# Sliding-window score products over 96 and 100 rows in place of 128 zero-padded rows

## The chip, the cores and the metric

The kernel runs on one core of one Trainium2 chip. A core has five engines with their own instruction streams: TensorE (PE in the profile: matmuls, with its weight loads listed apart as PEld), VectorE (DVE), ScalarE (ACT), GpSimd (POOL), and SyncE (SP), which here issues most DMA transfers. The metric is the device time of one execution in microseconds.

## The reference: what is computed

The input x has 2048 positions of 512 features. Two branches are computed from it and mixed by a gate.

```
a = real(DFT_seq(DFT_hidden(x)))                 # two dense matrix products, real part
q, k, v = x @ wqkv                               # 32 heads of 16
scores = q k^T / 4, masked to 0 <= query - key < 256
b = softmax(scores) @ v, heads joined, @ wo
g = sigmoid(sum(x * gate_w))
out = g * a + (1 - g) * b
```

All numbers are float32.

## The kernel before, in words

A float32 operand x is split into hi, its rounding to the matmul's own format (fp32r), and lo = x - hi; a product is then the sum of hi·hi, hi·lo and lo·hi. The dense products (projections of q, k and v in lines 259 to 313, the hidden DFT in line 320, the sequence DFT in line 520, and the output product in line 785) run these three terms as three matmuls of 128x128 weights against 512 columns.

The attention does the three terms in one matmul, by stacking them along the contracted rows. The 32 heads are worked in four groups, each with four pairs of heads. For a pair there are 32 features (two heads of 16). Two large tiles, called rings, hold 2048 positions for the four pairs: ring 0 holds queries, scaled and with the sign turned, with rows 0 to 31 hi, 32 to 63 lo and 64 to 95 hi again; ring 1 holds keys with rows 0 to 31 hi, 32 to 63 hi and 64 to 95 lo. The 96 rows thus give hi·hi + lo·hi + hi·lo. `ring_load` (line 286) fills 512 positions of both rings with four DMA transfers from a scratch in DRAM.

For a block n of 64 positions, `make_pad` (line 334) builds the stationary operand from a ring: a pad holds the 64 positions twice, once with the rows of one head of the pair and zeros in those of the other, and once the other way round, so that its 128 columns are two heads times 64 positions. `s_pair` (line 353) multiplies a pad of queries with a window of ring 1, at most 320 keys; DVE adds the mask and takes the row extreme (line 365), ACT takes the exponential and its sum (line 368). These give each query's extreme and sum. `t_pair` (line 432) later multiplies a pad of keys with a window of ring 0, at most 320 queries, which gives the scores transposed; the extremes of the two heads are brought back by DMA into rows 96 to 99 of ring 0 (`m_ring`, line 401, hi and lo for two heads), and rows 96 to 99 of the key pads hold ones for the head that a column belongs to, so that the matmul itself takes the extreme into the score. ACT takes the exponential (line 446), POOL clears what lies outside the window (lines 450 and 454), and `pv` (line 457) multiplies with the values in plain float32, in four column strips of the array (128x32 each).

In the kernel before, both score products read all 128 rows of pad and ring. Rows that hold nothing must then be zero. There are two pads of queries, two of keys, and the two rings:

- The query pads' rows 96 to 127 are cleared once by POOL (`affine_select` in line 203). It reads a split tile of x only to have something to read; the result is zero throughout.
- The rings' rows 96 to 127 are cleared by POOL in eight pieces of 512 positions (`clear_rows`, line 197, called ahead of the loop and at n = 1, 3 and 5).
- The key pads' rows 96 to 127 are set to one by POOL and multiplied on DVE by the columns of `mrow` (`clear_pads`, line 209, called at n = 7). `mrow` is one in rows 96 and 97 for one head, 98 and 99 for the other, and zero elsewhere, so rows 100 to 127 become zero.

The order of PE's work is written out in the program: the loop over n (line 844) issues `s_pair` of block n for the four pairs, `t_pair` of block n - 19, and between them `fill` takes pieces of the stream of dense work (`dense`, line 586), so that one score product stands between every two or three dense matmuls. After the loop the rest of the dense work follows, then the output product. The order of POOL and of most of DVE and ACT is set by a scheduler from the program's dependencies, within the bounds of `behind` (a given instruction stays after another). The first loads and splits of the program (from line 144) are in a written order on DVE, ACT and SP.

Of the kernel before, what the change touches and what calls it, by code (L numbers as in the profile page):

```python
# [10 lines left out]
OP = mybir.AluOpType  # L11
# [3 lines left out]
P = 128  # L15
# [4 lines left out]
NP = 4  # L20
# [12 lines left out]
def fnet_window_mix(ctx: ExitStack, tc: tile.TileContext, xT, x, wqk, wv, wr, wi, cr, ci, wo, gw, out):  # L33
    nc = tc.nc
# [23 lines left out]
    def f(ap):  # L58
        return ap.bitcast(F32)
# [4 lines left out]
    def mark(e, ins):  # L64
        last[e] = ins.ins

    @contextmanager
    def behind(*engines):
        with ExitStack() as es:
            for e in engines:  # L70
                if e in last:
                    es.enter_context(tc.issue_after(last[e]))
            yield
# [50 lines left out]
    XT = {}  # L124
# [17 lines left out]
    with tc.manual_schedule(engines={mybir.EngineType.Activation, mybir.EngineType.DVE, mybir.EngineType.SP}):  # L142
# [12 lines left out]
        for dk in range(DK):  # L155
            c = slice(dk * 256, dk * 256 + 256)
# [6 lines left out]
    pads = [[const.tile([P, NP, P], F32R, name=f"pad{i}_{b}") for b in range(NPAD)] for i in range(2)]  # L163
    ring = [const.tile([P, NP, S], F32R, name=f"ring{i}") for i in range(2)]
# [3 lines left out]
    for h in (0, 64):  # L168
        m = mask[h:h + 64, :]
        nc.gpsimd.affine_select(m, m, pattern=[[1, WIN]], compare_op=OP.is_gt, fill=BIG,  # L170
                                base=0, channel_multiplier=-1)
        nc.gpsimd.affine_select(m, m, pattern=[[-1, WIN]], compare_op=OP.is_ge, fill=BIG,
                                base=256, channel_multiplier=1)
# [3 lines left out]
                            base=0, channel_multiplier=-1)  # L177
# [3 lines left out]
    mrow = const.tile([P, 2], F32, name="mrow")  # L181
    for t, edges in ((half, ((0, 16, 32, 48, 64, 80), (16, 32, 48, 64, 80, 96))), (mrow, ((96, 98), (98, 100)))):
        nc.gpsimd.memset(t, 0.0)
        for h in range(2):
            for i, e in enumerate(edges[h]):
                a = t[:, h:h + 1]
                nc.gpsimd.affine_select(a, a, pattern=[[0, 1]], compare_op=OP.is_ge, fill=1.0 - i % 2,
                                        base=e - 1, channel_multiplier=-1)
# [5 lines left out]
    def turned(t):  # L194
        return t[:].rearrange("x p (r h) -> x p r h", h=2)

    def clear_rows(i, ss):
        with behind("pool"):
            nc.gpsimd.memset(f(ring[i][96:128, :, ss * 512:(ss + 1) * 512]), 0.0)

    first_lo = f(XT[0, 0][96:128, 1]).rearrange("r (p c) -> r p c", p=NP)
    for t in pads[0]:
        mark("pool", nc.gpsimd.affine_select(t[96:128], first_lo, pattern=[[0, NP], [0, P]], compare_op=OP.is_gt,
                                             fill=0.0, base=0, channel_multiplier=0))
    clear_rows(1, 0)
    clear_rows(0, 0)
    vpad = [const.tile([P, 4, NP, 32], F32, name=f"vpad{b}") for b in range(2)]

    def clear_pads():
        for t in pads[1]:  # L210
            nc.gpsimd.memset(f(t[96:128]), 1.0)
            for h in range(2):
                a = turned(t)[96:128, :, :, h]
                nc.vector.tensor_scalar(a, f(a), mrow[96:128, h:h + 1], None, op0=OP.mult)


    gl = const.tile([P, 16], F32, name="gl")
# [114 lines left out]
    PAD = {}  # L332

    def make_pad(i, n):
        if not 0 <= n < NG * NB:
            return
        t = pads[i][n % NPAD]
        b = n % NB
        with behind(*(("act", "dve") if n < NPAD else ())):
            for h in range(2):  # L340
                src = f(ring[i][:96, :, b * BQ:(b + 1) * BQ])
                dst = turned(t)[:96, :, :, h] if i else t[:96, :, 64 * h:64 * h + 64]
                if i and h:
                    nc.scalar.activation(dst, src, AF.Copy, scale=half[:96, h:h + 1])  # L344
                else:
                    nc.vector.tensor_scalar(dst, src, half[:96, h:h + 1], None, op0=OP.mult)  # L346
        PAD[i, n] = t
# [5 lines left out]
    def s_pair(n, p):  # L353
        j = n % NB
        u, jj = divmod(n, 8)
        if jj == 0 and p == 0:
            ML[u] = at.tile([P, 2, NP * 8], F32, name="ml")
        nm, l = ML[u][:, 0], ML[u][:, 1]
        k0 = max(0, (j - 4) * BQ)
        w = (j + 1) * BQ - k0  # L360
        c = slice(p * 8 + jj, p * 8 + jj + 1)
        ps = ps_a.tile([P, 512], F32, name="s", tag="st")
        nc.tensor.matmul(ps[:, :w], PAD[0, n][:, p], ring[1][:, p, k0:k0 + w], start=True, stop=True)  # L363
        sm = at.tile([P, WIN], F32, name="sm", bufs=3)
        mark("dve", nc.vector.tensor_tensor_reduce(out=sm[:, :w], in0=ps[:, :w], in1=mask[:, WIN - w:],  # L365
                                                   scale=1.0, scalar=3e38, op0=OP.add, op1=OP.min,
                                                   accum_out=nm[:, c]))
        mark("act", nc.scalar.activation(sm[:, :w], sm[:, :w], AF.Exp, bias=nm[:, c], scale=-1.0,  # L368
                                         accum_out=l[:, c]))
# [52 lines left out]
    def v_spread(n):  # L422
        if n >= NG * NB:
            return
        raw = VR.pop(n)
        v2 = vpad[n // 4 % 2]
        for h in range(2):
            nc.gpsimd.tensor_scalar(v2[:, :, :, 16 * h:16 * h + 16], raw.rearrange("r j (p d) -> r j p d", d=16),  # L428
                                    side[:, h:h + 1], None, op0=OP.mult)
        V2[n // 4] = v2  # L430

    def t_pair(n, p):
        q0 = n % NB * BQ
        w = min(WIN, S - q0)
        if p == 0:
            if "proj" in have:
                more.append(n)
            c = (n - more[0]) % 6 * NP * WIN if more else 3072
            if c + NP * WIN <= 3072:
                PT[n] = f(home[:, c:c + NP * WIN].rearrange("p (a b) -> p a b", a=NP))  # L440
            else:
                PT[n] = at.tile([P, NP, WIN], F32, name="pt", bufs=4)
        pt = PT[n]
        ps = ps_a.tile([P, 512], F32, name="t", tag="st")
        nc.tensor.matmul(ps[:, :w], PAD[1, n][:, p], ring[0][:, p, q0:q0 + w], start=True, stop=True)  # L445
        nc.scalar.activation(pt[:, p, :w], ps[:, :w], AF.Exp, scale=-1.0)  # L446
        if p % 2:
            ph = slice(p - 1, p + 1)
            a = pt[:, ph, 0:64]
            nc.gpsimd.affine_select(a, a, pattern=[[0, 2], [2, 64]], compare_op=OP.is_ge, fill=0.0,  # L450
                                    base=1, channel_multiplier=-1)
            if w == WIN:
                a = pt[:, ph, 256:320]
                nc.gpsimd.affine_select(a, a, pattern=[[0, 2], [-2, 64]], compare_op=OP.is_gt, fill=0.0,  # L454
                                        base=-1, channel_multiplier=1)
# [352 lines left out]
    def ring_ahead(n):  # L808
        nonlocal loaded
        while loaded < 16:  # L810
            g, ss = divmod(loaded, 4)
            if n >= 32 * g + 8 * ss:
                need(("qk", g, ss))
            if ("qk", g, ss) not in have or n - LAG < 32 * (g - 1) + 8 * ss + 9:
                break
            with behind(*(("sp",) if g == 0 else ())):
                ring_load(g, ss)
            loaded += 1
# [18 lines left out]
    def v_next(n):  # L837
        if n < N:
            for c in range(2):
                need(("v", n % NB // 2 + c))  # L840
            with behind(*(("sp",) if n < 8 else ())):
                v_load(n)

    for n in range(N + LAG + 1):
        if n in (1, 3, 5):
            for i in range(2):
                clear_rows(1 - i, (n + 1) // 2)
        if n == 7:
            clear_pads()
        k = n - LAG  # L850
        ring_ahead(n + 1)
        if k in (-1, 4):
            v_spread(0 if k < 0 else 4)
        if k in (-4, -1, 4):
            v_next({-4: 0, -1: 4, 4: 8}[k])
        if n == 0:
            make_pad(0, 0)
        for p in range(NP):
            if n < N:
                s_pair(n, p)  # L860
            fill(n)
            if 0 <= k < N:
                t_pair(k, p)
            if p == 0:
                make_pad(0, n + 1)
                if k >= -1:
                    make_pad(1, k + 1)
            fill(n)
            for at_n, at_p, do in TURN:
                u, j = divmod(n - at_n, 8)  # L870
                if p == at_p and j == 0 and 0 <= u < 16:
                    do(u)
            if p == 3 and k % 8 == 6 and 0 <= k < N:
                l_load(k // 8)
            if p == 0 and full:
                o_out()
            if p == 2 and (k - summed >= (5 if more else 3) or k == N):
                for j in range(summed, k):
                    pv(j)
                summed = k  # L880
            if p == 3 and 4 * spread - 5 < summed and 4 * spread < N and n >= fresh:
                v_spread(4 * spread)
                spread += 1
                v_next(4 * spread)
                fresh = n + 2
# [49 lines left out]
```

## Time and profile before

| what | value |
|---|---|
| three runs | 858.51, 852.27 and 853.18 us, median 853.18 |
| the profiled execution | 854.57 us, with a span of 852.9 us from first to last instruction |
| PE busy | 844.8 us (99% of the span), 5166 matmuls |
| PEld busy | 691.3 us (81%) |
| DVE, ACT, POOL busy | 615.8, 593.7 and 251.9 us |
| score products, lines 363 and 445 | 512 each, mean 308 and 301 ns |
| mean granted clock of TensorE | 1.00 |

The profile is of one execution. A row of a group has the line of the program, engine, operation, what it writes and reads, the shape and the count; then busy time and mean duration, then the idle time just ahead of it on its engine. In PE's rows "128*128" is active rows times active columns of the array. Matmuls overlap in the array: one starts while the one before it still drains, so the time that a matmul takes from PE is read from its start to the next one's start, and not from its duration. In a timeline, rows of a kind that follow on each other are merged into one with a count, and idle time is in brackets with what ended it.

### The profile page before, as it was taken

The page shows a single profiled execution, that of the slowest core. Times are in us where ns is not written, and L with a number is a line of the kernel's source. Part 1 is how long each engine was busy: PE and PEld are TensorE (multiplying, and loading weights), DVE is VectorE, ACT ScalarE, POOL GpSimd, SP SyncE. Part 2 cuts the span into 40 slices and gives each one's busy share as a digit, 9 for nine tenths or more (in the row PEclk, how much of TensorE's full clock was granted, in tenths as well). Part 3 has the DMA queues.
Part 4 walks back from the last instruction along what each step waited for, and adds up shares of the span by engine and source line. Part 5 has one row for each costly group of instructions (what it writes and reads, how often), then busy time and mean ns, then how long its engine had stood idle before and what let it go on. Part 6 is the DMA issues. An engine that isn't in the chain of part 4 may idle for free.

```text
span 852.9 us, 16687 instructions
## 1 busy us (share of the span) xinstructions
PE 844.8 (99%) x5166; PEld 691.3 (81%) x5166; DVE 615.8 (72%) x2013; ACT 593.7 (70%) x1793; POOL 251.9 (30%) x585
## 2 busy tenths in 40 slices
PE   9999999999999999999999999999999999999998
PEld 7788788788788888888878887888888887877887
DVE  5588978667878787669777787788888774437531
ACT  5388798878888987779878897778777765532200
POOL 9000222333332333333423324333243354510000
PEclk9999999999999999999999999999999999999999
DMA  7876578576675275444435557989784344359542
GB/s 255 276 235 201 172 247 249 198 236 210 205 249 181 59 210 127 152 125 143 148 120 145 164 144 216 286 278 292 242 225 140 117 153 144 124 176 303 158 147 98
DMA packets 94344, 160.99 MB, mean 189 GB/s; under 512 B 26800, under 2 KB 35760, under 8 KB 94256
## 3 DMA queue, kind: packets, MB, share of 16 engines
q1 hardware_dynamic: 93824, 159.28, 59.8%
q8 instruction: 40, 0.66, 0.3%
q10 hardware_dynamic: 432, 0.66, 0.2%
q14 instruction: 48, 0.39, 0.1%
HBM read 108.27 MB, written 51.64 MB: 187 GB/s over the span
## 4 chain that ended last, share of the span: by engine, by line
PE 92%; DMA 4%; DVE 2%; ACT 1%; issue 1%; SPq 0%; DVEq 0%; ACTq 0%
PE dc L523 39%; PE dab L300 10%; PE s L363 9%; PE t L445 8%; PE o L471 8%; PE dqk L277 8%; PE t L793 5%; PE dv L300 4%; DMA raw<-xT 1%; DMA fin<-o_scr 1%; DMA o_scr<-ev 1%; DVE sm L365 1%; DMA pt<-wqk 0%; DVE big L81 0%; SPq L56 0%
## 5 line engine op out<-in xcount | busy, mean ns | idle before, releaser
L368 ACT ACTIVATE sm<-sm,ml 128x320 f32<-128x320 f32 (+4 forms) x512 | 277.9, 544 | 101.1 <-DVE ml L365 96.4
L523 PE MATMUL dc<-big,hi 128*128 128x512 f32 x1020 | 344.4, 393 | 0.0
L365 DVE CUSTOM_DVE_ANT_0 sm<-s,mask 128x320 f32<-128x320 f32 (+4 forms) x512 | 235.3, 464 | 113.2 <-PE s L363 91.5
L523 PE MATMUL dc<-big,lo 128*128 128x512 f32 x510 | 200.6, 393 | 0.0
L523 PEld LDWEIGHTS dc<-big,hi 128*128 128x128 f32 x1020 | 179.7, 188 | 21.4
L446 ACT ACTIVATE pt<-t 128x320 f32<-128x320 f32 (+4 forms) x392 | 160.3, 411 | 43.0 <-PE t L445 40.9
L450 POOL TENSOR_SCALAR_AFFINE_SELECT pt<-pt 128x128 f32<-128x128 f32 x196 | 72.2, 368 | 302.0 <-ACT pt L446 299.8
L363 PE MATMUL s<-ring,pad 128*128 128x320 f32 (+4 forms) x512 | 157.7, 308 | 0.0
L445 PE MATMUL t<-ring,pad 128*128 128x320 f32 (+4 forms) x512 | 154.1, 301 | 0.1
L346 DVE TENSOR_SCALAR pad<-ring,half 96x256 fp32r<-96x256 f32 x384 | 119.9, 358 | 13.5 <-PE t L445 13.3
L363 PEld LDWEIGHTS s<-ring,pad 128*128 128x128 f32 x512 | 96.1, 188 | 30.3 <-issue 9.0
L445 PEld LDWEIGHTS t<-ring,pad 128*128 128x128 f32 x512 | 96.1, 188 | 22.0 <-DVE ml L365 1.0
L523 PEld LDWEIGHTS dc<-big,lo 128*128 128x128 f32 x510 | 95.9, 188 | 13.8 <-issue 1.6
L368 ACT ACTIVATION_READ_ACCUMULATOR sm<-sm,ml 128x1 f32 x512 | 97.7, 191 | 0.0
L428 POOL TENSOR_SCALAR vpad<-vr,half 128x256 f32<-128x256 f32 x64 | 60.5, 958 | 124.9 <-DMA vr<-v_scr 75.7
L579 DVE TENSOR_TENSOR lo<-raw,hi 128x512 fp32r<-128x512 f32 x142 | 96.8, 691 | 0.1
L300 PE MATMUL dab<-hi,big 128*128 128x512 f32 x256 | 89.2, 394 | 0.0
L277 PE MATMUL dqk<-big,hi 128*128 128x512 f32 x240 | 85.7, 394 | 1.5 <-DVE big L81 0.9
L579 DVE CAST hi<-raw 128x512 fp32r<-128x512 f32 x142 | 60.1, 432 | 18.7 <-PE dc L523 13.0
L344 ACT ACTIVATE pad<-ring,half 96x256 fp32r<-96x256 f32 x128 | 66.6, 520 | 0.0
L454 POOL TENSOR_SCALAR_AFFINE_SELECT pt<-pt 128x128 f32<-128x128 f32 x172 | 62.0, 361 | 0.1
L446 ACT ACTIVATE home<-t 128x320 f32<-128x320 f32 (+4 forms) x120 | 49.0, 408 | 13.4 <-PE t L445 11.5
(97 smaller groups left out, 915.3 us busy)
## 6 DMA issues: line engine op xcount, KB each, us to landing
qk_scr<-home SPq DMA_DIRECT2D x32, 512.0 KB
ring<-qk_scr SPq DMA_DIRECT2D x32, 512.0 KB
raw<-cr SPq DMA_DIRECT2D x32, 512.0 KB
raw<-ci SPq DMA_DIRECT2D x32, 512.0 KB
r_scr<-ev SPq DMA_DIRECT2D x42, 256.0 KB
ev<-r_scr SPq DMA_DIRECT2D x42, 256.0 KB
ab_scr<-home SPq DMA_DIRECT2D x20, 512.0 KB
big<-ab_scr SPq DMA_DIRECT2D x20, 512.0 KB
```

Source lines behind the costliest of these rows:

```text
L277: nc.tensor.matmul(ps, w[a][:, c:c + 128], XT[dk, ss][:, b], start=n == 0, stop=n == 11)
L300: nc.tensor.matmul(ps, XT[dk, ss][:, a, c * 128:(c + 1) * 128], wh[b], start=n == 0, stop=n == 11)
L346: nc.vector.tensor_scalar(dst, src, half[:96, h:h + 1], None, op0=OP.mult)
L363: nc.tensor.matmul(ps[:, :w], PAD[0, n][:, p], ring[1][:, p, k0:k0 + w], start=True, stop=True)
L365: mark("dve", nc.vector.tensor_tensor_reduce(out=sm[:, :w], in0=ps[:, :w], in1=mask[:, WIN - w:], scale=1.0, scalar=3e38, op0=OP.add, op1= ...
L368: mark("act", nc.scalar.activation(sm[:, :w], sm[:, :w], AF.Exp, bias=nm[:, c], scale=-1.0, accum_out=l[:, c]))
L445: nc.tensor.matmul(ps[:, :w], PAD[1, n][:, p], ring[0][:, p, q0:q0 + w], start=True, stop=True)
L446: nc.scalar.activation(pt[:, p, :w], ps[:, :w], AF.Exp, scale=-1.0)
L450: nc.gpsimd.affine_select(a, a, pattern=[[0, 2], [2, 64]], compare_op=OP.is_ge, fill=0.0, base=1, channel_multiplier=-1)
L471: nc.tensor.matmul(OT[g, sb][32 * p:32 * p + 32, q - sb * 512:e - sb * 512], v2[:, p], pt[:, p, q - q0:e - q0], start=first, stop=kb == 8 ...
L523: nc.tensor.matmul(ps, w[a][:, i % 8 * 128:i % 8 * 128 + 128], ab[SC[i]][:, b], start=i == ends[0] and a + b == 0, stop=i == ends[1] and a ...
L579: return fn(*args)
```

## The change

The score products read 96 rows of query pad and ring 1 (`s_pair`), and 100 rows of key pad and ring 0 (`t_pair`). Nothing reads the other rows any more, so the clearing of the query pads and of both rings is taken out, and that of the key pads is cut to rows 96 to 99.

```diff
-    def clear_rows(i, ss):
-        with behind("pool"):
-            nc.gpsimd.memset(f(ring[i][96:128, :, ss * 512:(ss + 1) * 512]), 0.0)
-
-    first_lo = f(XT[0, 0][96:128, 1]).rearrange("r (p c) -> r p c", p=NP)
-    for t in pads[0]:
-        mark("pool", nc.gpsimd.affine_select(t[96:128], first_lo, pattern=[[0, NP], [0, P]], compare_op=OP.is_gt,
-                                             fill=0.0, base=0, channel_multiplier=0))
-    clear_rows(1, 0)
-    clear_rows(0, 0)
...
         for t in pads[1]:
-            nc.gpsimd.memset(f(t[96:128]), 1.0)
+            nc.gpsimd.memset(f(t[96:100]), 1.0)
             for h in range(2):
-                a = turned(t)[96:128, :, :, h]
-                nc.vector.tensor_scalar(a, f(a), mrow[96:128, h:h + 1], None, op0=OP.mult)
+                a = turned(t)[96:100, :, :, h]
+                nc.vector.tensor_scalar(a, f(a), mrow[96:100, h:h + 1], None, op0=OP.mult)
...
-        nc.tensor.matmul(ps[:, :w], PAD[0, n][:, p], ring[1][:, p, k0:k0 + w], start=True, stop=True)
+        nc.tensor.matmul(ps[:, :w], PAD[0, n][:96, p], ring[1][:96, p, k0:k0 + w], start=True, stop=True)
...
-        nc.tensor.matmul(ps[:, :w], PAD[1, n][:, p], ring[0][:, p, q0:q0 + w], start=True, stop=True)
+        nc.tensor.matmul(ps[:, :w], PAD[1, n][:100, p], ring[0][:100, p, q0:q0 + w], start=True, stop=True)
...
-        if n in (1, 3, 5):
-            for i in range(2):
-                clear_rows(1 - i, (n + 1) // 2)
```

In the changed program PE, ACT and SP have the same instructions in the same order, apart from the rows. The four multiplies of `clear_pads` on DVE, which the scheduler places, move from behind the splits of the second quarter of x to just behind the first split of the first weights (line 159).

## The prediction

> **What bounds the kernel now.** I read the page first (span, busy slices, chain of waits), then the busy time by stretches, then the order of instructions in time where the kinds of product meet.
>
> ```profile
> span 852.9 us, 16687 instructions
> PE   9999999999999999999999999999999999999998
> PEclk9999999999999999999999999999999999999999
> PE 92%; DMA 4%; DVE 2%; ACT 1%; issue 1%; SPq 0%; DVEq 0%; ACTq 0%
> L363 PE MATMUL s<-ring,pad 128*128 128x320 f32 (+4 forms) x512 | 157.7, 308 | 0.0
> L445 PE MATMUL t<-ring,pad 128*128 128x320 f32 (+4 forms) x512 | 154.1, 301 | 0.1
> ```
>
> ```profile
> 0.00:35.00 35.00, 32.21 (x129) 25.38 (x130) 19.35 (x38) 13.97 (x25) 21.84 (x41) 1.00 0.85 282
> 119.00:340.00 221.00, 221.00 (x1440) 180.13 (x1440) 172.91 (x599) 186.64 (x580) 70.25 (x176) 1.00 0.61 192
> 340.00:689.00 349.00, 349.00 (x2282) 287.86 (x2281) 275.38 (x958) 273.19 (x856) 116.63 (x276) 1.00 0.60 183
> ```
>
> The columns of the second view are the length of the stretch, then busy time and count of PE, PEld, DVE, ACT and POOL, the granted clock, the DMA share and GB/s. In the two long stretches that hold most of the attention PE has no idle time, at a granted clock of 1.00; DVE and ACT sit at 78% and 84% of 119 to 340 us (172.91 and 186.64 of 221). So the kernel ends when PE has got through its list, and a change counts by what it adds to or takes from PE's slots. The exception is the first 26 us, where PE waits for inputs. The 1024 score products (512 in line 363, 512 in line 445) are what the change touches on PE. Their durations overlap, so their price must be read from starts:
>
> ```profile
> 126.90 0.31 PE L363 MATMUL s<-ring,pad 128*128 128x320 f32 x1
> 127.04 0.39 PE L300 MATMUL dab<-hi,big 128*128 128x512 f32 x1
> 127.27 0.39 PE L300 MATMUL dab<-lo,big 128*128 128x512 f32 x1
> 127.50 0.31 PE L445 MATMUL t<-ring,pad 128*128 128x320 f32 x1
> 127.64 0.62 PE L300 MATMUL dab<-hi,big 128*128 128x512 f32 x2
> ```
>
> A score product of 320 columns holds PE for 0.14 us (126.90 to 127.04, and 127.50 to 127.64), a dense one of 512 for 0.23 us. That is 0.44 and 0.45 ns a column: the slot goes with the moving columns, which the change leaves alone.
>
> **The change part by part.** The changed program has the same matmuls in the same order on PE; 512 of them have 96 rows and 512 have 100 in place of 128, and all 1024 keep the 128x128 tile at position 0, with the same moving columns and the same 128 stationary columns. The issues of SP and ACT are the same and in the same order, so no transfer passes another.
>
> *(a) 1024 products of fewer rows.* The trace has no product or weight load with fewer than 128 rows, so this is the unknown price. Bound from below: if a slot went with its rows, it would fall by 0.14 x 32/128 = 0.035 us for 512 of them and by 0.14 x 28/128 = 0.031 us for the other 512, 34 us in all. Nothing excludes that; the slots above follow columns, but at one number of rows. For the bound from above there are two places where another number of active columns enters PE:
>
> ```profile
> 133.87 0.39 PE L300 MATMUL dab<-hi,big 128*128 128x512 f32 x1
> 133.88 0.36 PEld L383 LDWEIGHTS s<-ident,mlh 128*64 128x64 f32 x2
> 134.10 0.28 PE L383 MATMUL s<-ident,mlh 128*64 128x128 f32 x2
> 134.22 0.36 PE L363 MATMUL s<-ring,pad 128*128 128x320 f32 x1
> ```
>
> ```profile
> 118.42 0.67 PE L300 MATMUL dab<-hi,big 128*128 128x512 f32 x2
> 119.02 1.82 PE L471 MATMUL o<-pt,vpad 128*32 128x320 f32 x24
> 120.77 0.41 PE L363 MATMUL s<-ring,pad 128*128 128x320 f32 x1
> 121.02 0.39 PE L300 MATMUL dab<-lo,big 128*128 128x512 f32 x1
> ```
>
> In the first, from 128*128 to 128*64 and back, the weights of the small product load while the dense product streams (133.88, just after 133.87); the dense product takes its usual 0.23 us, and the two small ones of 128 columns take 0.12 us together, 0.06 each, by columns again. This border costs nothing. In the second, from 128*128 to 128*32 with plain f32 operands, two dense products take 0.60 us (118.42 to 119.02) where 0.46 is usual, 0.14 us more; on the way back the score product holds PE for 0.25 us where 0.14 is usual, 0.11 us more. There the next weights were not loaded under the product in flight. Paying 0.14 + 0.11 at both borders of each of 1024 products would be 512 us: the upper end. I take zero, by the first border: it is nearest, since it keeps the operands' type and the same place in the array, as the change does, and changes only how much of the array is active.
>
> The Trainium skill ("TensorEngine Tiling (Array Packing)", Key Properties) says that changing the tiling mode, not just the tile, drains the array. By that rule the 128*64 border ought to drain as well, and this trace shows it does not; the 128*32 border agrees. The page's modes have 128, 64 or 32 rows, so 96 and 100 rows would stay in the 128-row mode and the rule would give no change; were 96 rows a mode of their own, it would give the 512 us of the upper end. The skill also says ("TensorE: Matmul & The Clock Gate", LDWEIGHTS) that a weight load costs by columns and a 32-row load takes as long as a 128-row one; no run here shows that yet, and it would give zero too.
>
> *(b) Clearing that goes.* POOL loses the eight ring clears and the two selects that clear the first pads.
>
> ```profile
> 5.86 0.32 POOL L187 TENSOR_SCALAR_AFFINE_SELECT mrow<-mrow 128x1 f32<-128x1 f32 x2
> 6.25 1.23 POOL L203 TENSOR_SCALAR_AFFINE_SELECT pad<-big 32x512 fp32r<-32x512 f32 x2
> 7.42 14.09 POOL L199 MEMSET ring<- 32x2048 f32 x8
> 21.85 0.32 POOL L187 TENSOR_SCALAR_AFFINE_SELECT mrow<-mrow 128x1 f32<-128x1 f32 x2
> ```
>
> ```profile
> L363 PE MATMUL s<-ring,pad x512: 191/310/418, 35.0 to 688.1; 128*128 128x320 f32 x149, 128*128 128x64 f32 x6, 128*128 128x256 f32 x6, 128*128 128x128 f32 x5
> ```
>
> These 15 us end at 21.5 us; the first score product is at 35 us and waits on loads into its ring, so the clears are hidden and their going is worth zero in itself.
>
> *(c) The key pads' multiplies move on DVE.* There are still four of 256 elements a row, now on 4 rows instead of 32; I price them the same, since the elements in a row set the work. Their inputs (mrow, line 187) come earlier because POOL is free, and they move from 24.9 us to DVE's place just after its first line 159:
>
> ```profile
> 5.45 0.42 DVE L159 TENSOR_TENSOR lo<-pt,hi 128x256 fp32r<-128x256 f32 x1
> 6.94 1.07 DVE L81 TENSOR_TENSOR big<-pt,big 128x512 fp32r<-128x512 f32 x1 [1.08 <-ACT big L78]
> ...
> 8.28 0.68 DVE L81 TENSOR_TENSOR big<-pt,big 128x512 fp32r<-128x512 f32 x1
> ```
>
> ```profile
> 11.46 3.57 DMA raw<-xT
> ...
> 24.92 0.35 DVE pad L214
> ...
> 25.31 0.70 DVE big L81
> ...
> 26.05 3.47 PE dqk L277 x14
> ```
>
> In the changed order the multiplies wait for the second pair of mrow selects. These end 0.66 us after the clears (22.17 against 21.51), and now follow at once on the first pair, which ends at 6.18: about 6.8 us. Four multiplies of up to 0.35 us end at about 8.1. Queued behind them is the split of line 81 that began at 6.94, for which PE waits: 1.2 us late. It took 1.07 us beside POOL's selects against 0.68 for the next, so without them it gets 0.39 back: 0.8 us late. The splits behind it stand close, and the raw buffer that the transfer at 11.46 refills is freed by the last of them, so the delay runs along this chain (views: DVE's order in time, then the chain of waits). Further on, the 0.35 us multiply between two splits (0.39 us from its start to the next split's) has gone. Net: +0.8 - 0.4 = +0.4 us at 26.05, where PE takes over and carries it to the end. Bounds: -0.8 if all of the wait is hidden (0.39 + 0.39), +1.2 if nothing is given back.
>
> **Sum.** 0 (a) + 0 (b) + 0.4 (c): a span of 853.3 us against 852.9. The profiled execution took 854.57 us, 1.4 more than the median of the three runs, 853.18; against the median I forecast **853.6 us**.
>
> **Rivals.**
>
> *Weights not loaded ahead (slower).* If PE does not load weights for another number of rows while a product streams, the load is exposed at each entry, as at 120.77. Place: each of the 1024 products; price: 0.11 us, 113 us, 967 us. For it: that border exists. Against: 128*64 shows no such thing. It decides from 8 ns a product (8.5 us).
>
> *Drain at both borders (slower).* Entry and exit both pay, 0.11 to 0.25 us each: +225 to +512 us, 1079 to 1366 us. Same evidence, and a stronger claim.
>
> *A small fee (slower).* Something of 0.01 to 0.03 us a product, too small for the starts to show at the 128*64 border: +10 to +31 us, 864 to 885 us.
>
> *Rows count (faster).* The lower bound of (a): up to 34 us, 820 us; half of it, 837 us, if only one of weight load and stream shortens. Against it: the weight loads follow columns, and lie under the stream anyway:
>
> ```profile
> L445 PEld LDWEIGHTS t<-ring,pad 128*128 128x128 f32 x512 | 96.1, 188 | 22.0 <-DVE ml L365 1.0 <-PE s L363 0.3
> L383 PEld LDWEIGHTS s<-ident,mlh 128*64 128x64 f32 x32 | 4.3, 134 | 3.1 <-DVE mlh L377 1.0
> ```
>
> A load of 188 ns for 128 columns against 134 for 64 is a matter of columns, and shortening it would save nothing where 0.23 us of streaming covers it.
>
> **How the numbers follow.** No change 0.52 (851.5 to 856 us: the bounds of (c), and some of the spread of the three runs); small fee 0.12; weights not ahead 0.17; drain at both borders 0.13; rows count 0.06. One per cent, 8.5 us, is about what a measurement of this kernel can tell from no change. Faster by over 1%: 0.06; within: 0.52; slower: 0.42. The range takes in the first three and leaves out 0.19: 851 to 970 us. So wide a range comes from (a) alone, as no row has another number of rows; the likeliest case's own is 851.5 to 856.
>
> **What would show it.** Right: a score product of 320 columns still 0.14 us from start to start with 96 and with 100 rows, a dense one before and after it 0.23, weight loads of 188 ns that start with the product before. Wrong in (a): a dense product of 0.3 us or more ahead of a score product, weight loads of s or t that start when the array is empty, PEld idle before lines 353 and 435 (now 363 and 445), and so fewer products in each stretch from 35 us on. If 96 rows cost and 100 do not, the cost goes with whole strips of 32 rows. Step (c) is right if DVE's multiplies stand near 7 us, the split behind them starts near 8.1, and the first idle time of PE after 24 us ends within 1 us of 26.05. A granted clock under 1.00 would upset all of it.

## The result, and the profile after

The changed kernel takes 864.37 us (median of four runs, 863.97 to 864.98); the kernel before, beside it, 853.84. The ratio is 1.0125, with a 95% interval of 1.0101 to 1.0149: 1.25% slower, some 10.5 us. The time lies inside the range of 851 to 970 us, but no change was forecast, and there is one. The profiled execution took 864.2 us with a span of 862.5.

The page of the kernel after, with the rows that answer to those of before:

```profile
span 862.5 us, 16677 instructions
PEclk9999999999999999999999999999999999999999
PE 94%; DMA 2%; DVE 2%; issue 1%; POOL 1%; ACT 0%; POOLq 0%; DVEq 0%; ACTq 0%
L353 PE MATMUL s<-ring,pad 96*128 96x320 f32 (+4 forms) x512 | 159.0, 310 | 0.1
L435 PE MATMUL t<-ring,pad 100*128 100x320 f32 (+4 forms) x512 | 155.6, 304 | 0.3 <-DVE ml L355 0.3
L353 PEld LDWEIGHTS s<-ring,pad 96*128 96x128 f32 x512 | 96.0, 187 | 30.9 <-issue 9.0
```

The clock is still full, PE bounds the kernel as before, and these rows show no new wait of any size. A weight load of 96 rows takes 187 ns where one of 128 took 188. The stretches (columns as in the prediction: length, then busy time and count of PE, PEld, DVE, ACT, POOL) say that PE is busy throughout, and gets less done:

```profile
119.00:340.00 221.00, 221.00 (x1423) 178.78 (x1423) 170.31 (x589) 184.72 (x571) 68.63 (x172) 1.00 0.60 192
340.00:689.00 349.00, 348.52 (x2252) 284.72 (x2251) 270.69 (x940) 268.82 (x840) 112.88 (x270) 1.00 0.59 179
```

1423 matmuls where there were 1440, and 2252 where there were 2282: 1.2 and 1.3% fewer in the same time. PE's order in time shows where; one period of two score products and four dense ones:

```profile
127.11 0.31 PE L353 MATMUL s<-ring,pad 96*128 96x320 f32 x1
127.25 0.40 PE L290 MATMUL dab<-hi,big 128*128 128x512 f32 x1
127.49 0.40 PE L290 MATMUL dab<-lo,big 128*128 128x512 f32 x1
127.72 0.31 PE L435 MATMUL t<-ring,pad 100*128 100x320 f32 x1
127.88 0.63 PE L290 MATMUL dab<-hi,big 128*128 128x512 f32 x2
128.34 0.31 PE L353 MATMUL s<-ring,pad 96*128 96x320 f32 x1
```

From 127.11 to 128.34 the period takes 1.23 us. In the kernel before the same period ran from 126.90 to 128.10 (its last row follows), 1.20 us. No slot has a gap that could be pointed at: 0.03 us are spread over six.

```profile
128.10 0.31 PE L363 MATMUL s<-ring,pad 128*128 128x320 f32 x1
```

To add this up, take the stretch from the first untransposed score product to the last transposed one, which the rows by line give (first and last start). The first row is of before; the start of line 363, 35.0, stands in the prediction.

```profile
L445 PE MATMUL t<-ring,pad x512: 191/310/414, 100.9 to 763.4; 128*128 128x320 f32 x150, 128*128 128x128 f32 x6, 128*128 128x256 f32 x5, 128*128 128x192 f32 x5
```

```profile
L353 PE MATMUL s<-ring,pad x512: 195/312/417, 34.3 to 697.8; 96*128 96x320 f32 x149, 96*128 96x64 f32 x6, 96*128 96x256 f32 x6, 96*128 96x128 f32 x5
L435 PE MATMUL t<-ring,pad x512: 195/313/413, 100.6 to 774.1; 100*128 100x320 f32 x150, 100*128 100x128 f32 x6, 100*128 100x256 f32 x5, 100*128 100x192 f32 x5
```

Before: 763.4 - 35.0 = 728.4 us. After: 774.1 - 34.3 = 739.8 us, 11.4 us more, or 11 ns for each of the 1024 score products. The whole span grew by 9.6 us. Of the 1.8 us between, 0.7 is the earlier start (34.3 against 35.0) and 1.1 lie behind the last score product (88.4 us to the end against 89.5). There the chain of waits of before ran through transfers, and the output product in line 793 began only when its split was there, after 0.59 us in which PE was idle:

```profile
777.73 4.90 DMA fin<-o_scr
782.66 0.63 ACT os L78
783.33 22.54 PE t L793 x96
```

In the kernel after, PE doesn't wait there, and the chain is of products alone:

```profile
777.39 16.13 PE dc L513 x70
793.52 21.97 PE t L783 x96
```

This isn't because PE comes later. The split behind these transfers (line 78) is done 18.6 us after the last score product begins, and 19.9 us after it in the kernel before; PE is ready for it 19.2 to 19.4 us after it in both. So the transfers move with PE. In st127 below PE is 10 us late as well and still waits, for 0.63 us, and in all100, 0.8 us late, it doesn't. The wait comes and goes from one profiled execution to another.

The first 26 us are the place of the multiplies on DVE. DVE's order in time, and PE's, after:

```profile
6.63 1.20 DVE L204 TENSOR_SCALAR pad<-pad,mrow 4x256 fp32r<-4x256 f32 x4 [0.76 <-POOL mrow L187]
7.85 0.69 DVE L81 TENSOR_TENSOR big<-pt,big 128x512 fp32r<-128x512 f32 x1
```

```profile
8.60 0.73 PE L255 MATMUL s<-big,hi 128*128 128x512 f32 x2 [0.88 <-DVE big L81]
```

### The profile page after: what moved, and what is told of

It is laid out like the page before. It is cut to its first block, busy times and chain, and to the rows that moved or that the text cites. A ratio compares the mean times of both kernels' runs of the same rounds, so it can differ in the third digit from the quotient of the medians.

```text
span 862.5 us, 16677 instructions
## 1 busy us (share of the span) xinstructions
PE 855.0 (99%) x5166; PEld 695.8 (81%) x5166; DVE 615.7 (71%) x2013; ACT 596.2 (69%) x1793; POOL 234.8 (27%) x575
## 4 chain that ended last, share of the span: by engine, by line
PE 94%; DMA 2%; DVE 2%; issue 1%; POOL 1%; ACT 0%; POOLq 0%; DVEq 0%; ACTq 0%
PE dc L513 41%; PE dab L290 10%; PE s L353 8%; PE dqk L267 8%; PE t L435 8%; PE o L461 8%; PE dv L290 5%; PE t L783 5%; DMA raw<-cr 1%; DMA qk_scr<-home 1%; DVE sm L355 1%; PE s L255 0%; ACT sm L358 0%; DVE pad L336 0%; DVE home L88 0%
## 5 line engine op out<-in xcount | busy, mean ns | idle before, releaser
L513 PE MATMUL dc<-big,hi 128*128 128x512 f32 x1020 | 348.2, 396 | 0.0
L513 PEld LDWEIGHTS dc<-big,hi 128*128 128x128 f32 x1020 | 182.0, 190 | 23.8
L353 PE MATMUL s<-ring,pad 96*128 96x320 f32 (+4 forms) x512 | 159.0, 310 | 0.1
L435 PE MATMUL t<-ring,pad 100*128 100x320 f32 (+4 forms) x512 | 155.6, 304 | 0.3 <-DVE ml L355 0.3
L440 POOL TENSOR_SCALAR_AFFINE_SELECT pt<-pt 128x128 f32<-128x128 f32 x196 | 70.2, 358 | 310.3 <-ACT pt L436 308.1
L353 PEld LDWEIGHTS s<-ring,pad 96*128 96x128 f32 x512 | 96.0, 187 | 30.9 <-issue 9.0
L435 PEld LDWEIGHTS t<-ring,pad 100*128 100x128 f32 x512 | 96.0, 187 | 22.7 <-DVE ml L355 1.3
L444 POOL TENSOR_SCALAR_AFFINE_SELECT pt<-pt 128x128 f32<-128x128 f32 x172 | 61.9, 360 | 0.0
```

What stands on the lines that cost most here:

```text
L353: nc.tensor.matmul(ps[:, :w], PAD[0, n][:96, p], ring[1][:96, p, k0:k0 + w], start=True, stop=True)
L435: nc.tensor.matmul(ps[:, :w], PAD[1, n][:100, p], ring[0][:100, p, q0:q0 + w], start=True, stop=True)
L513: nc.tensor.matmul(ps, w[a][:, i % 8 * 128:i % 8 * 128 + 128], ab[SC[i]][:, b], start=i == ends[0] and a + b == 0, stop=i == ends[1] and a ...
```

## The experiments

Each theory below says where 11 ns a product come from. *Border*: a change of the number of active rows from one product to the next costs PE some 5 ns, in either direction. *Narrow*: a product of fewer rows costs more by itself. *Clearing*: the time comes from the clears that went and from what moved with them. All kernels start from the kernel before and keep its clears. The "stretch" is first to last score product, as above, of one profiled execution each; it is free of the start and of the end, but not of waits in between. Where the number of active rows changes, it changes back soon after, so every run has as many changes to fewer rows as to more, and none tells what one direction costs.

| run | products with another number of active rows (or columns) than most of their neighbours | ratio to before, 95% interval | stretch, against 728.4 us | per product |
|---|---|---|---|---|
| changed kernel | 1024 | 1.0125 (1.0101 to 1.0149) | +11.4 | 11 ns |
| pe_only | 1024 | 1.0103 (1.0088 to 1.0118) | +10.2 | 10 ns |
| s96 | 512 | 1.0074 (1.0059 to 1.0089) | +6.2 | 12 ns |
| t100 | 512 | 1.0075 (1.0058 to 1.0091) | +6.7 | 13 ns |
| all100 | none of the score or dense products | 1.0003 (0.9993 to 1.0013) | +0.8 | |
| dense100 | 1024 (the score products, in the midst of 100 rows) | 1.0115 (1.0091 to 1.014) | +10.5 | 10 ns |
| st127 | 1024 | 1.0099 (1.008 to 1.0119) | +11.1 | 11 ns |
| s96_p0 | 128 | 0.9997 (0.9984 to 1.001) | +1.7, of which 0.7 is a wait of PE | 8 ns without the wait |
| s64 | 512 (64 rows) | 1.2259 (1.2229 to 1.2289) | +194.9 | 381 ns |
| mid_rows96 | 733 dense ones in the stretch | 1.0109 (1.0065 to 1.0153) | +10.1 | 14 ns |
| mid_cols96 | 733, in columns | 1.0055 (1.0029 to 1.0081) | +4.9 | 7 ns |

**pe_only: the matmul lines alone.**

```diff
-        nc.tensor.matmul(ps[:, :w], PAD[0, n][:, p], ring[1][:, p, k0:k0 + w], start=True, stop=True)
+        nc.tensor.matmul(ps[:, :w], PAD[0, n][:96, p], ring[1][:96, p, k0:k0 + w], start=True, stop=True)
...
-        nc.tensor.matmul(ps[:, :w], PAD[1, n][:, p], ring[0][:, p, q0:q0 + w], start=True, stop=True)
+        nc.tensor.matmul(ps[:, :w], PAD[1, n][:100, p], ring[0][:100, p, q0:q0 + w], start=True, stop=True)
```

> The kernel before with only the two matmul lines changed (96 and 100 rows); all clears stay as they were. Border theory (a change of active rows between neighbouring products costs about 5 ns at each border) and narrow theory (a product of fewer rows costs about 10 ns itself): about 10 us above the kernel before, 863 to 865 us. Clearing theory (the time comes from the clears that went and the multiplies that moved): 853 to 854.5 us.

862.81 us, a ratio of 1.0103. With every clear in place and DVE's order unchanged, nearly the whole loss is there. The clearing theory falls; what the clears and the moved multiplies add or take is inside the overlap of the two intervals.

**s96 and t100: one of the two lines each.** The edits are the first and the second pair of lines above.

> The kernel before with only the 512 untransposed score products at 96 rows, all clears kept. Border and narrow theory: half of the loss, +4 to +6 us, 857.5 to 860 us. If only a partly used strip of 32 rows costs (100 rows, not 96): no change, 853 to 854.5 us.

> The kernel before with only the 512 transposed score products at 100 rows, all clears kept. Border and narrow theory: half of the loss, +4 to +6 us, 857.5 to 860 us. If only a partly used strip of 32 rows costs: the whole loss, 863 to 865 us.

860.56 and 860.42 us. Both lose about the same, so a partly used strip of 32 rows (100 is three strips and four rows) is not what costs, and neither is the transposed product as such. By the stretch each has a little over half of the loss (6.2 and 6.7 of 11.4 us); the two add up to 12.9 us, more than both at once cost in pe_only (10.2). So the price of a border isn't quite fixed. Nor is the time lost at the border alone. In s96 the transposed products have 128 rows between dense products of 128 rows, and still their row has a median duration of 314 ns, where before, above, it had 310:

```profile
L445 PE MATMUL t<-ring,pad x512: 190/314/416, 100.7 to 769.1; 128*128 128x320 f32 x150, 128*128 128x128 f32 x6, 128*128 128x256 f32 x5, 128*128 128x192 f32 x5
```

Counted along PE's order from start to start, where all neighbours are dense products and PE doesn't wait, they hold PE for 142.0 ns on average in place of 137.4 before, 4.6 ns more; the narrow products themselves hold it for 140.8 in place of 138.1, 2.7 more. t100 has the same the other way round: 4.4 ns more for the products that kept 128 rows, 3.4 for the narrow ones.

**all100: the dense products at the same rows as the score products.** Six matmul calls are cut to `[:100]` in both operands besides the two above, such as:

```diff
-                nc.tensor.matmul(ps, w[a][:, i % 8 * 128:i % 8 * 128 + 128], ab[SC[i]][:, b],
+                nc.tensor.matmul(ps, w[a][:100, i % 8 * 128:i % 8 * 128 + 128], ab[SC[i]][:100, b],
```

> The kernel before with every product of the 128-column kind at 100 rows, dense and score alike; rows 100 to 127 of the contraction are left out of the dense products. Border theory: score products have neighbours of the same rows, so the loss goes: 852 to 856 us. Narrow theory: some 3700 products pay about 10 ns each, 885 to 892 us.

854.27 us, a ratio of 1.0003: the loss is gone, with more narrow products than in any other run. PE's order in time, one period:

```profile
124.70 0.31 PE L363 MATMUL s<-ring,pad 100*128 100x320 f32 x1
...
125.30 0.31 PE L445 MATMUL t<-ring,pad 100*128 100x320 f32 x1
...
125.90 0.31 PE L363 MATMUL s<-ring,pad 100*128 100x320 f32 x1
```

1.20 us, as with 128 rows throughout. The narrow theory falls here: 100 rows cost nothing as long as the neighbours have 100 too.

**dense100: the reverse.** The same six calls at 100 rows, the score products at 128.

> The reverse: all dense products at 100 rows (rows 100 to 127 of their contraction are left out), the score products at 128, clears kept. Border theory: as many borders as in the changed kernel, so about the same loss, 862 to 866 us. If a border cost only on the way into fewer rows, or only at the score products' own short slots, 857 to 860 us.

865.28 us. The loss is back, with the narrow and the full products exchanged. It has 2198 narrow products in the stretch and about the same number of borders as the changed kernel (2056 against 2046, counted along PE's order), and it loses about the same (10.5 against 11.4 us): the time goes with the number of borders and not with that of narrow products, at 5 to 6 ns a border on average. The second answer that was written down can't be told from the first here: with as many borders into fewer rows as in the changed kernel, a price in that direction alone would give the whole loss again.

**st127: one row fewer.** As pe_only, with 127 in both places.

> Both score products at 127 rows, one fewer than the dense ones, clears kept. If any change of the number of active rows costs: 862 to 865 us as with 96 and 100. If the cost goes with the rows left out or with whole strips of 32 rows: 853 to 855 us.

864.6 us, +11.1 us in the stretch. The size of the step doesn't matter; that the number changes does.

**s96_p0: an eighth of the borders.**

```diff
+        x = 96 if p == 0 else P
-        nc.tensor.matmul(ps[:, :w], PAD[0, n][:, p], ring[1][:, p, k0:k0 + w], start=True, stop=True)
+        nc.tensor.matmul(ps[:, :w], PAD[0, n][:x, p], ring[1][:x, p, k0:k0 + w], start=True, stop=True)
```

> Only the untransposed score product of the first of four head pairs at 96 rows (128 products of 1024; one narrow product to some 23 of full rows), clears kept. Fee theory (a fixed price at each border): an eighth of the loss, +1.2 to +1.6 us, 855 to 856 us. Rhythm theory (a border throws PE out of a fast rhythm of starts, and the slower one lasts for many products): near to what 512 narrow products cost, +4 to +6 us, 858 to 860 us.

855.0 us, a ratio of 0.9997 (0.9984 to 1.001, which is -1.4 to +0.9 us). No loss can be measured, and the +1.2 to +1.6 us of the fee theory lie above the interval. The stretch has +1.7 us, but 0.69 of them are one wait of PE, for a row extreme of DVE at 548.5 us, that the kernel before doesn't have. The 1.0 us that is left is hardly more than the +0.8 us of all100, where dense and score products have the same rows, so this run doesn't show what a lone narrow product costs. PE's order in time, around one of them:

```profile
207.45 0.31 PE L364 MATMUL s<-ring,pad 128*128 128x320 f32 x1
...
208.65 0.31 PE L364 MATMUL s<-ring,pad 96*128 96x320 f32 x1
...
209.87 0.30 PE L364 MATMUL s<-ring,pad 128*128 128x320 f32 x1
```

The period ahead of the narrow product takes 1.20 us, the one that begins with it 1.22. A rhythm that once lost stays lost for many products would have cost +4 to +6 us; that theory falls. In s96 the delay reaches products three places from the border; over the 23 full products between narrow ones here no such loss can be measured.

**s64: 64 rows, another tile.** `[:64]` in the first matmul line alone.

> The 512 untransposed score products at 64 rows (the term with the keys' lo part is left out), which the program places in a 64x128 tile in place of 128x128; the rest at 128 rows, clears kept. If a change of tiling mode drains the array as at the 128*32 border (0.14 us in, 0.11 us out): +56 to +128 us, 910 to 982 us or more. If it costs what 96 rows cost: +4 to +7 us, 858 to 861 us.

1048.03 us, a ratio of 1.2259. 0.38 us a product, more than the 0.11 us of the prediction's exposed load and within what its rival of a drain at both borders would cost (two times 0.11 to 0.25 us). PE's order in time, and the weight load of the narrow product:

```profile
149.86 0.39 PE L300 MATMUL dab<-lo,big 128*128 128x512 f32 x1
150.09 0.39 PE L300 MATMUL dab<-hi,big 128*128 128x512 f32 x1
150.41 0.41 PE L363 MATMUL s<-ring,pad 64*128 64x320 f32 x1
150.75 0.50 PE L300 MATMUL dab<-hi,big 128*128 128x512 f32 x1
151.09 0.39 PE L300 MATMUL dab<-lo,big 128*128 128x512 f32 x1
```

```profile
150.40 0.18 PEld L363 LDWEIGHTS s<-ring,pad 64*128 64x128 f32 x1 [0.36 <-issue]
```

In the changed kernel the load of 96 rows starts with the dense product ahead (both at 126.88), 0.23 us before its own product at 127.11:

```profile
126.88 0.19 PEld L353 LDWEIGHTS s<-ring,pad 96*128 96x128 f32 x1
```

With 64 rows the load starts 0.31 us behind the dense product ahead (150.40 against 150.09), beside the score product itself.

The dense product ahead takes 0.32 us in place of 0.23, the score product 0.34 in place of 0.14, the dense one behind it 0.34: 0.09 + 0.20 + 0.11 = 0.40 us. The expectation, from single borders, had nothing for the score product itself, where half of the cost lies; why it lies there is not shown. The Trainium skill ("TensorEngine Tiling (Array Packing)", Key Properties) says that a change of tiling mode drains the array. The trace agrees for 64 rows, which the page lists as a mode; 96, 100 and 127 rows are none of its modes, and at 10 to 14 ns a product the runs show no such pause for them.

**mid_rows96 and mid_cols96: away from the score products, and columns in place of rows.** The middle one of each dense product's three terms is narrowed, in three calls such as these (rows, then columns):

```diff
+                x = 96 if (a, b) == (0, 1) else P
-                nc.tensor.matmul(ps, w[a][:, i % 8 * 128:i % 8 * 128 + 128], ab[SC[i]][:, b],
+                nc.tensor.matmul(ps, w[a][:x, i % 8 * 128:i % 8 * 128 + 128], ab[SC[i]][:x, b],
```

```diff
+                x = 96 if (a, b) == (0, 1) else P
-                nc.tensor.matmul(ps, w[a][:, i % 8 * 128:i % 8 * 128 + 128], ab[SC[i]][:, b],
+                nc.tensor.matmul(ps[:x], w[a][:, i % 8 * 128:i % 8 * 128 + x], ab[SC[i]][:, b],
```

> The kernel before with the middle of each dense product's three terms at 96 rows (its rows 96 to 127 are left out); 822 narrow products, each between two of 128 rows; score products at 128 rows. Border theory, at the 11 to 13 ns a narrow product that the earlier runs gave: 9 to 11 us more on PE, about 1 of it given back at the end, 862 to 866 us. If only the score products' short slots are sensitive: 853 to 856 us.

> The same 822 products narrowed in columns in place of rows: 96 of 128 stationary columns, so output rows 96 to 127 lack the middle term; 128 rows throughout. If a change in how much of the array is active costs, in either direction: 862 to 866 us, as with rows. If rows alone matter: 853 to 856 us.

865.37 us with rows, 859.99 with columns. The cost isn't bound to the score products: a narrow one among the dense ones costs 14 ns (10.1 us for 733). The profiled run of mid_rows96 began its first score product 3.5 us late. PE had waited 2.20 us for a split, until 27.75 us, and the granted clock was 0.91 from 25 to 30 us and 0.75 from 30 to 35, where the kernel before, has 1.00 with a wait of 0.91 us. The stretch begins behind that. And columns cost as well, about half as much, 7 ns a product. Neither of the two answers that were written down for mid_cols96 fits: it is slower than before by more than its interval, and less than with rows. One dense triple at the end, far from any score product, before:

```profile
815.23 0.62 PE L523 MATMUL dc<-big,hi 128*128 128x512 f32 x2
815.68 0.39 PE L523 MATMUL dc<-big,lo 128*128 128x512 f32 x1
815.91 0.62 PE L523 MATMUL dc<-big,hi 128*128 128x512 f32 x2
```

With the middle term of 96 rows:

```profile
819.41 0.62 PE L526 MATMUL dc<-big,hi 128*128 128x512 f32 x2
819.87 0.40 PE L526 MATMUL dc<-big,lo 128*128 128x512 f32 x1
820.11 0.63 PE L526 MATMUL dc<-big,hi 128*128 128x512 f32 x2
```

0.68 us a triple before, 0.70 with rows narrowed.

No run points to a version faster than both kernels: the borders can be taken away by 128 rows everywhere, and that is the kernel before.

## Why the prediction was wrong

The range of 851 to 970 us holds the measured time, but only because it takes in the slower rivals. The forecast of 853.6 us and no change failed, and so did the step that it rests on.

*(a), 1024 products of fewer rows: the step that failed.* "I take zero, by the first border." The border to 128*64 was read at a resolution of 0.01 us, and a fee of 5 to 6 ns is below that. It was also read on the way in alone. The row behind it is

```profile
134.42 0.39 PE L300 MATMUL dab<-hi,big 128*128 128x512 f32 x1
```

so the score product behind the two small ones, which began at 134.22, held PE for 0.20 us, and not for the usual 0.14 (0.18 on average at 15 such places). "This border costs nothing" thus fits the way in alone. Whether those 0.06 us come from the border, or from the weight loads of 0.19 us behind two products that take 0.06 us each, this trace doesn't tell. And mid_cols96 shows that a change of active columns from 128 to 96 is not free either (7 ns a product). With 1024 products and two borders each, what can't be read at one place is 11 us in the sum. The prediction itself said that the first slower rival decides from 8 ns a product, and gave a fee of "0.01 to 0.03 us" its own case, 864 to 885 us, with a chance of 0.12. That case came, at its lower edge. The taken value should have been "below 10 ns a border", which is anywhere from 0 to 20 us, and not zero. The upper end has a slip as well: the 128*32 border showed 0.14 us on the way in and 0.11 on the way out, which is 0.25 us a product and 256 us in all; the 512 us count both at each border.

*The reasons around it held.* Slots go with the moving columns, not with rows (all100: 1.20 us a period with 100 rows as with 128), so the rival on the faster side was rightly small. Weights are loaded ahead across a border of rows (the load at 126.88 above, and slots that grow by nanoseconds), so the exposed load and the drain were rightly set aside for 96 and 100 rows; s64 shows what they would have looked like.

*(b), the clears: right, as far as can be measured.* pe_only, with all of them in place, has a ratio of 1.0103 (1.0088 to 1.0118) against 1.0125 (1.0101 to 1.0149) without them: going away, they gave nothing that can be measured.

*(c), the moved multiplies: right at the start, not borne out at 26 us.* They began at 6.63 us, waited for the mrow selects as forecast, and the split behind them began at 7.85 where 8.1 was forecast, with 0.69 us in place of 1.07, as forecast for a split without POOL's clears of the pads beside it. PE's product that waits for it began at 8.60, 0.5 us late (8.07 before). Of the forecast 0.4 us at 26 us nothing is left. PE's wait of 0.91 us before, which ended at 26.05, is gone: the same product began at 25.51 without one, against the sign that was written down for (c), and the first score product began 0.7 us earlier than before. But in kernels whose clears and multiplies are those of before it began at 33.8 (t100), 34.3 (pe_only), 34.5 (s96) and 35.0 (all100), and the wait near 26 us is missing in t100 and pe_only as well, so one execution can't tell a step of this size. It stays open.

*The end.* That PE carries what it has at 26 us "to the end" was not quite so: PE can wait for the output product's split there, and kernels with this wait take 1.1 us longer from the last score product to the end (89.5 us before, 89.6 in st127) than those without (88.4 after and in all100).

*Chances.* Slower by over 1% had 0.42 and no change 0.52; what came is 1.25% slower.

## What to carry to other kernels

When PE has no idle time, a price that is too small to see in one slot must be bounded by its resolution times its count before it is set to zero. Keep the number of active rows the same from one matmul to the next where products of different kinds alternate; rows of zeros are cheap if the clears are hidden. A slot is best compared over a period of the program (here six products), since the excess is spread over the neighbours. Before a difference of 1 us between two traces is given a cause, look for single waits in both.

## What the hardware showed that was not expected

- A change of active rows from one product to the next, inside one tile size, costs 5 to 7 ns a border on average where products of different rows alternate throughout, about the same for 127, 100 and 96 rows (10 to 14 ns a narrow product in seven kernels, and +0.8 us in all where dense and score products have 100 rows alike). With one narrow product to some 23 full ones (s96_p0) no loss could be measured. Part of the time is lost at products that have no border themselves (s96, t100). Why is not settled: weight load and product always changed their rows together, and no view shows what PE does in those nanoseconds.
- A change of active columns from 128 to 96 and back costs about half, 7 ns a product, in one kernel.
- A change to 64 rows and back costs 0.38 us a product, thirty times as much, and the weights are not loaded ahead.
- After one wait of PE of 2.20 us in mid_rows96 the granted clock was 0.91 and then 0.75 in the two stretches of 5 us from 25 us on, and 1.00 from 35 us; whether the wait was the reason is not shown.
